# Scores as four wide row tiles, an output projection in 64-row pairs, and new orders, in a two-layer attention and MLP kernel

## The chip, the cores and the metric

The kernel runs on one core of a Trainium2 chip. The metric is the device time of one execution in microseconds (us). The kernel before was timed three times, and the median counts. A profile of one further execution gives, for every instruction, when it began and how long it took. TensorE (PE in the profile, its weight loads PEld) multiplies matrices into PSUM; VectorE (DVE), ScalarE (ACT) and GpSimd (POOL) do the rest; SyncE (SP) issues the DMAs.

## The reference

```
x = x + A(layernorm(x));  x = x + B(layernorm(x))      # both twice, with the same weights
A: qkv = x @ wqkv                    # 2048 x 576 by 576 x 1728, 32 heads of 18
   scores = q k^T * 18**-0.5         # key within the last 256 positions, causal
   p = softmax(scores);  o = p v;  return o @ wo       # wo: 576 x 576
B: y = layernorm(x);  h = gelu(y @ w1 + b1)            # w1: 576 x 4608
   return h @ w2 + b2                                  # w2: 4608 x 576
```

There are 2048 tokens of 576 features, in bf16.

## The kernel before, in words

The 16 token tiles of 128 are taken four at a time, so that each of the two layers has four chunks; the chunks are numbered k = 0 to 7. For each chunk the stages are: the first layernorm and a transposed copy of the activations (`ln1`, `ln_norm_T`), Q, K and V (`qkv`), attention in eight head groups of four heads (`E`, with `scores` and `pv`), the output projection with residual and second layernorm (`tail`), and the MLP in three parts (`G_part` for the first matrix with GELU, `mm2` for the second). The stages of neighbouring chunks are interleaved.

**Tilings of TensorE.** Four shapes are used. QKV of chunks 2 and later and the first MLP matrix run as pairs: two matmuls of 64 rows x 128 columns side by side, on the lower and the upper half of the rows, each into its own PSUM bank (lines 838 and 1077; mode `h`). They run in two phases of 5 and 4 chunks of rows; in the second the halves swap banks, and a flag `own` makes it wait until the first has finished. The second MLP matrix and the output projection use all 128 rows (`two_out`, `quad`; mode `c`): full 128x128 matmuls (line 779), or four 128x32 ones side by side (line 782) where they share a stretch with the product of probabilities and V (`pv`, line 957), which uses that tiling. The scores (line 908; mode `r`) use 32 rows, since a head has 18 features padded to 32: for each of the four heads of a group two matmuls of 32 rows x 64 columns, eight side by side, called a volley in this text. One unit of scores has 512 columns in one or two volleys, for chunks 0 and 4 partly less; a group of four heads has three units. ScalarE takes the exponential (line 919), GpSimd masks the corner blocks (line 940).

**Output projection.** The attention output `attq` holds four head families of 144 features each on the four partition quarters. VectorE transposes it in 32-column chunks into `attT` (line 978). Of the fifth chunk only 16 of 32 columns are real; the rest is set to zero once, as is the fifth chunk of the weights `wo_sb`. So the projection of one token tile takes five row chunks for each of two output halves of 288 columns.

**Order.** The instructions aren't in the order in which the code names them. A planner (`Plan.schedule`) holds a task for each piece of work with an assumed cost, its engine, a priority and what it reads and writes. It takes, again and again, the task that can begin first; among those that begin alike the one with the lowest priority number. A table, `PL.nudge`, adds a number to the priority of every stage and part. A change of tiling on TensorE is charged 0.095 us, and `PL.turn` holds back a task of another tiling by up to 0.3 us. The order so found is fixed in the program for every engine, the DMA queue of SP included. Where TensorE would stand idle early on, the planner puts in zero matmuls (`keep_warm`, line 681); it divides the planned gap by 0.115 us for each.

**Ramp.** Until the first MLP matmul, at 89 us, there is only the attention of chunks 0 and 1 and QKV of chunks 0 to 2. The results of QKV are copied out of PSUM by VectorE (lines 859 and 846), for Q and K of chunk 0 half by ScalarE (line 856). The normalisation ahead of each MLP (`xn`, line 719) is done by VectorE; GpSimd copies its last 64 columns once more (line 727), and a DMA transposes it into `xnTm` (line 742).

Of the kernel before, what the change touches and what calls it, by code (L numbers as in the profile page):

```python
# [7 lines left out]
ACT = mybir.ActivationFunctionType  # L8
# [178 lines left out]
class Plan:  # L187
# [21 lines left out]
    def add(self, eng, fn, reads=(), writes=(), dma=None, ring=4, cost=0.1, lat=0.1, prio=0.0, alloc=(), fifo=None, plain=False, after=(), move=0.0, desc=0, hold=False, mode="f", own=False, port=None, wide=None):  # L209
# [3 lines left out]
        prio += self.nudge.get(stage, 0.0)  # L213
# [35 lines left out]
    def keep_warm(self, a, b, bank_free, extra):  # L249
# [3 lines left out]
        n = int((b - a - 0.1) * 0.8 / 0.115)  # L253
# [5 lines left out]
        t = Task(idx=-1, eng="pe", fn=lambda e: self.warm_fn(e, h.no, n), reads=("warm",), writes=(h,), cost=n * 0.115, lat=0.1, prio=0.0,  # L259
# [175 lines left out]
def build_kernel(nc, A_x, A_wqkv, A_wo, B_x, B_w1, B_b1, B_w2, B_b2, out):  # L435
# [42 lines left out]
    PL.nudge = {"": -58.92, "b": 20.48, "ea0.0": -239.22, "ea0.1": 16.47, "ea0.2": -7.62, "ea0.p0": -24.76, "ea0.p1": -56.2,  # L478
# [105 lines left out]
    def bank(i):  # L584
        if isinstance(i, Bank):
            i = i.no
        return ps[:, i * 512:(i + 1) * 512]
# [123 lines left out]

    xn_ctr = [0]

    def ln_norm_T(t, i, dst, dname, prio, src=None, srcres=None, dup=False, pe=False):
# [602 lines left out]
```

## Time and profile before

| | |
|---|---|
| time, median of 3 runs | 874.53 us (872.73 to 874.58) |
| the profiled execution: span from first to last instruction | 871.0 us |
| what lies around the span, against the median | 3.5 us |
| TensorE busy | 854.1 us (98%), 13464 matmuls |
| its weight loads | 533.0 us |
| ScalarE, VectorE, GpSimd busy | 595.7, 392.3, 376.8 us |
| granted TensorE clock, in 40 slices | 9 tenths or more in each |
| DMA | 120 MB, mean 138 GB/s |

For the profiled execution the span is all that the profile tells of its own time. The span runs from the first instruction to the last; the time of a run has a little more around it. Busy time is the union over an engine's instructions. Matmuls overlap (one of 288 columns is on record for 0.287 us, and the next begins 0.12 us later), so that what a matmul costs TensorE is read from the distance of the starts, not from its length. A row of the timeline has the start, the length from the first start to the last end, the engine, the line, what is written and read, the tiling (rows*columns) and shape, and the count; in brackets stands the idle time before it. A row of groups has, after the bar, busy us and mean ns of one, and then the idle time before, with what ended it. "issue" is waiting for nothing that the profile shows.

### The profile page before, as it was taken

To read this page: it belongs to the slowest core of one execution; us is meant where nothing else is said; L and a number is where in the kernel's file an instruction comes from. 1 tells how busy PE (TensorE), PEld (TensorE's weight loads), DVE (VectorE), ACT (ScalarE), POOL (GpSimd) and SP (SyncE) were. 2 spreads that over 40 slices of the span, in tenths; PEclk is the share of its full clock that TensorE was granted. 3 is DMA by queue.
4 is the path that set the end of the run, shared out by engine and by line. 5 is a ranking of instruction groups with operands and counts; after the bars stand their busy time and mean duration, and the time that the engine had idled before them with its cause. 6 is when DMAs were issued, how large, how long until landed. Compare 5 with 4: busy or idle time off the path is not lost.

```text
span 871.0 us, 30752 instructions
## 1 busy us (share of the span) xinstructions
PE 854.1 (98%) x13464; PEld 533.0 (61%) x13464; DVE 392.3 (45%) x934; ACT 595.7 (68%) x741; POOL 376.8 (43%) x560
## 2 busy tenths in 40 slices
PE   8899999999999999999999999999999999999998
PEld 6556556666556665665655665756556656556556
DVE  4889324554327542384424822654234434234012
ACT  4986788768666588573875776737797589772730
POOL 3876454464144643254421763425454276222100
PEclk9999999999999999999999999999999999999999
DMA  9598435371574715947349453684526963445320
GB/s 238 137 201 143 121 124 149 102 166 44 165 161 118 170 43 164 203 91 166 88 145 222 99 129 124 103 186 99 172 93 136 280 147 105 138 149 156 123 82 28
DMA packets 181877, 120.01 MB, mean 138 GB/s; under 512 B 107440, under 2 KB 181744, under 8 KB 181744
## 3 DMA queue, kind: packets, MB, share of 16 engines
q1 hardware_dynamic: 181744, 118.05, 54.7%
q8 instruction: 106, 1.74, 0.8%
q14 instruction: 27, 0.22, 0.1%
HBM read 90.10 MB, written 2.36 MB: 106 GB/s over the span
## 4 chain that ended last, share of the span: by engine, by line
PE 90%; ACT 3%; DMA 3%; issue 2%; DVE 1%; POOL 0%; DVEq 0%; POOLq 0%
PE ps L1077 32%; PE ps L779 26%; PE ps L782 10%; PE ps L838 9%; PE ps L908 7%; PE ps L957 4%; ACT pT L919 3%; DMA xnTm<-xn 2%; PE ps L798 1%; PE ps L681 1%; DMA x_res<-qn 1%; DMA qT<-qn 1%; DVE xn L719 0%; DVE qn L859 0%; ACT hT L1087 0%
## 5 line engine op out<-in xcount | busy, mean ns | idle before, releaser
L940 POOL TENSOR_SCALAR_AFFINE_SELECT pT<-pT 128x512 bf16<-128x512 bf16 (+1 forms) x368 | 282.8, 789 | 262.8 <-ACT pT L919 260.2
L919 ACT ACTIVATE pT<-ps 128x1024 bf16<-128x1024 f32 (+1 forms) x384 | 347.5, 970 | 62.1 <-PE ps L908 61.1
L1077 PE MATMUL ps<-xnTm,w_sb 64*128 64x512 bf16 x2592 | 290.6, 376 | 2.9 <-DMA xnTm<-xn 2.4
L1087 ACT ACTIVATE hT<-ps,b1col 128x512 bf16<-128x512 f32 x276 | 167.6, 688 | 176.8 <-PE ps L1077 176.3
L1077 PEld LDWEIGHTS ps<-xnTm,w_sb 64*128 64x128 bf16 x2592 | 129.6, 94 | 143.7 <-issue 8.2
L779 PE MATMUL ps<-w_sb,hT 128*128 128x288 bf16 x1410 | 188.8, 287 | 0.0
L1020 DVE TENSOR_TENSOR x_res<-ps,x_res 128x288 f32<-128x288 f32 x224 | 100.2, 451 | 191.9 <-PE ps L779 163.2
L779 PEld LDWEIGHTS ps<-w_sb,hT 128*128 128x128 bf16 x1410 | 130.8, 98 | 47.5 <-issue 13.9
L782 PE MATMUL ps<-w_sb,hT 128*32 128x288 bf16 x2808 | 96.2, 286 | 0.8 <-issue 0.7
L838 PE MATMUL ps<-wqkv,xnTa 64*128 64x288 bf16 x1296 | 91.4, 283 | 0.9 <-DVE x_res L1020 0.6
L968 DVE STREAM_TRANSPOSE oq<-ps 128x512 f32<-128x512 f32 x64 | 45.7, 715 | 101.6 <-PE ps L957 100.8
L859 DVE CAST qn<-ps 128x288 bf16<-128x288 f32 x120 | 48.9, 451 | 81.4 <-PE ps L838 71.7
L782 PEld LDWEIGHTS ps<-w_sb,hT 128*32 128x32 bf16 x2808 | 72.4, 97 | 15.7 <-issue 5.0
L838 PEld LDWEIGHTS ps<-wqkv,xnTa 64*128 64x128 bf16 x1296 | 63.0, 94 | 28.3 <-issue 2.9
L908 PE MATMUL ps<-qT,kT 32*64 32x384 bf16 (+2 forms) x2432 | 69.1, 284 | 3.5 <-DMA qT<-qn 1.5
L694 DVE BATCH_NORM_STATS2 st_all<-x_res 128x6 f32<-128x288 f32 (+1 forms) x128 | 53.5, 443 | 6.9 <-DMA x_res<-in_A_x_dram 6.1
L1093 POOL TENSOR_TENSOR x_res<-x_res,b2bc 128x576 f32<-128x576 f32 x32 | 40.2, 1275 | 34.8 <-ACT hT L1087 34.8
L846 DVE CAST vA<-ps 128x288 bf16<-128x288 f32 x64 | 26.7, 451 | 61.1 <-PE ps L838 59.0
L707 POOL TENSOR_SCALAR vtmp<-mv_all 128x1 f32<-128x1 f32 (+1 forms) x43 | 8.8, 205 | 101.9 <-DVE mv_all L698 99.1
L908 PEld LDWEIGHTS ps<-qT,kT 32*64 32x64 bf16 x2432 | 25.4, 102 | 44.1 <-issue 29.4
L957 PE MATMUL ps<-pT,vA 128*20 128x384 bf16 (+2 forms) x1408 | 50.4, 275 | 1.2 <-POOL pT L940 0.6
L957 PEld LDWEIGHTS ps<-pT,vA 128*20 128x20 bf16 x1408 | 28.2, 91 | 18.1 <-issue 5.5
(58 smaller groups left out, 483.9 us busy)
## 6 DMA issues: line engine op xcount, KB each, us to landing
w_sb<-in_B_w_dram SPq DMA_DIRECT2D x46, 864.0 KB, 5.9
w_sb<-in_B_w_dram SPq DMA_DIRECT2D x48, 768.0 KB, 4.7
w_sb<-in_B_w_dram SPq DMA_DIRECT2D x96, 48.0 KB, 4.5
wqkv<-in_A_wqkv_dram SPq DMA_DIRECT2D x3, 576.0 KB, 5.5
x_res<-in_A_x_dram SPq DMA_DIRECT2D x3, 576.0 KB, 4.9
wqkv<-in_B_w_dram SPq DMA_DIRECT2D x2, 864.0 KB, 6.4
out_dram<-x_res SPq DMA_DIRECT2D x12, 144.0 KB, 2.0
wo_sb<-in_A_wo_dram SPq DMA_DIRECT2D x4, 144.0 KB, 2.6
```

What stands on the lines that cost most here:

```text
L694: add("dve", lambda e, i=i, s=s: e.bn_stats(st_all[:, t, i, :], s[:, t, i * HB:(i + 1) * HB]), reads=res, writes=[f"st{t}_{i}"], cost=0.37 ...
L779: return e.matmul(bank(b)[:, 0:HB], lhs, rhs, start=start, stop=stop, skip_group_check=True)
L782: ins = e.matmul(bank(b)[32 * j:32 * j + 32, 0:HB], lhs[:, 32 * j:32 * j + 32], rhs, start=start, stop=stop, tile_position=(0, 32 * j), sk ...
L838: ins = e.matmul(bank(bs[o])[:, 0:HB], xnTa[r:r + 64, c, i * 128:(i + 1) * 128], wqkv[r:r + 64, c, col:col + HB], start=(c == 4), stop=(ph ...
L859: add("dve", lambda e, b=bs[o], dst=dst: e.tensor_copy(dst, heads_of(bank(b))), reads=[bs[o]], writes=[f"qn{sl}h{o}"], cost=0.375, lat=0.1 ...
L908: ins = e.matmul(two(bs[j // 2])[64 * u:64 * u + 64, j % 2, col:col + nq * 128], k_of(T0 + so)[0][32 * j:32 * j + 32, g, 64 * u:64 * u + 6 ...
L919: add("act", lambda e, h2=h2: e.activation(pT[:, sl, 2 * h2:2 * h2 + 2, lo:hi], two(bs[h2])[:, :, lo:hi], ACT.Exp, scale=SCALE), reads=[bs ...
L940: add("pool", lambda e, ap=ap, pat=pat, sgn=sgn, kind=kind: e.affine_select(ap, ap, pattern=pat, compare_op=(ALU.is_ge if kind == "d" else ...
L957: ins = e.matmul(bank(bo)[32 * j:32 * j + VW, qo * 128:(qo + nq) * 128], vA[:, (T0 + so) % VS, 8 * j + g, :], pT[:, sl, j, col:col + nq * ...
L1020: add("dve", lambda e: e.tensor_tensor(x_res[:, t, sl], bank(b)[:, 0:HB], x_old[:, t, sl], ALU.add), reads=[b] + ([f"xin{t}"] if first els ...
L1077: ins = e.matmul(bank(bks[i])[:, 0:n], w1_sb[r:r + 64, sls[i], col:col + 128], xnTm[r:r + 64, k % 2, c, 0:n], start=(c == 4), stop=(ph == ...
L1087: add("act", lambda e, ff=ff, hd=hd, bk=bk: e.activation(hd[:, 0:n], bank(bk)[:, 0:n], ACT.Gelu_apprx_tanh, bias=b1col[:, ff:ff + 1]), rea ...
```

## The change

- **Scores:** for each head one matmul of 32 rows x 128 columns instead of two of 32x64. A volley is then four matmuls, and writes the same four PSUM banks.
- **Output projection:** pairs of 64x128 in two phases, as QKV does it. The fifth row chunk holds the 64 real features densely, twice: on the lower half for the first output half, on the upper half for the second. So the first phase has five pairs and the second four. VectorE makes the dense copy with four small copies after the last head group; the fifth chunk of the weights comes in eight DMAs instead of four, 12 in all instead of 8. Two memsets go.
- **Zero matmuls:** where a planned gap begins before 8 us, it is divided by 0.2 instead of 0.115.
- **Drains in the ramp:** in chunk 2 ScalarE copies the second half of Q, K and V out of PSUM. For the first MLP (chunk 0) it also does the normalisation, as scale and bias; GpSimd works out the bias first.
- **Orders:** all of `PL.nudge` has new numbers; priorities are rounded to three places.

```diff
@@ keep_warm
-        n = int((b - a - 0.1) * 0.8 / 0.115)
+        each = 0.2 if a < 8.0 else 0.115
+        n = int((b - a - 0.1) * 0.8 / each)
@@ build_kernel
-    PL.nudge = {"": -58.92, "b": 20.48, "ea0.0": -239.22, "ea0.1": 16.47, "ea0.2": -7.62, "ea0.p0": -24.76, "ea0.p1": -56.2,
...
+    PL.nudge = {"": -86.31, "b": 23.63, "ea0.0": -264.23, "ea0.1": 170.66, "ea0.2": 170.75, "ea0.p0": -91.12, "ea0.p1": 0.1, "ea0.p2":
...
-    add("pool", lambda e: e.memset(attq[:, :, 8 * DH:KD * 32], 0.0), writes=["aqd"], cost=0.5, prio=-8)
-    add("dve", lambda e: e.memset(wo_sb[:, 4, :], 0.0), writes=[f"woB{j}" for j in range(4)], cost=0.4, prio=-8)
@@ ln_norm_T
+        if onact:
+            add("pool", lambda e: e.tensor_scalar(vtmp[:, t:t + 1], mv_all[:, t, 0:1], rstd[:, t:t + 1], -1.0, op0=ALU.mult, op1=ALU.mult),
+                reads=[f"mv{t}", f"rstd{t}"], writes=[f"vt{t}"], cost=0.2, lat=0.09, prio=prio)
+            add("act", lambda e: e.activation(xn[:, sl, 0:D], s[:, t, :], ACT.Identity, bias=vtmp[:, t:t + 1], scale=rstd[:, t:t + 1]),
+                reads=res + [f"vt{t}", f"rstd{t}"], writes=[f"xn{sl}"], cost=0.56, lat=0.17, prio=prio)
@@ qkv
+                    if k == 2 and o == 1:
+                        add("act", lambda e, dst=dst, src=src: e.copy(dst, src()), reads=[bs[o]], writes=[f"v{sv}h{o}"], cost=0.32, lat=0.17, prio=prio)
...
-                    if k == 0 and o == 1:
+                    if k in (0, 2) and o == 1:
@@ scores
-                    for u in range(2):
-                        ins = e.matmul(two(bs[j // 2])[64 * u:64 * u + 64, j % 2, col:col + nq * 128],
-                                       k_of(T0 + so)[0][32 * j:32 * j + 32, g, 64 * u:64 * u + 64],
-                                       qs[32 * j:32 * j + 32, g, qo * 128:(qo + nq) * 128], start=True, stop=True, tile_position=(32 * j, 64 * u),
-                                       skip_group_check=True)
+                    ins = e.matmul(two(bs[j // 2])[:, j % 2, col:col + nq * 128], k_of(T0 + so)[0][32 * j:32 * j + 32, g, :],
+                                   qs[32 * j:32 * j + 32, g, qo * 128:(qo + nq) * 128], start=True, stop=True, tile_position=(32 * j, 0),
+                                   skip_group_check=True)
@@ pv
+        if g == G - 1:
+            for p0, p1, c0, w, q0 in ((0, 32, 16, 16, 32), (32, 64, 0, 16, 64), (32, 64, 16, 16, 96), (64, 128, 0, 32, 0)):
+                add("dve", lambda e, p0=p0, p1=p1, c0=c0, w=w, q0=q0: e.tensor_copy(attq[p0:p1, 0:4 * nt, 128 + c0:128 + c0 + w],
+                                                                                   attq[q0:q0 + p1 - p0, 0:4 * nt, 128:128 + w]),
+                    reads=[f"aq{g}"], writes=["aqd"], cost=0.2, lat=0.14, prio=prio - 3, port=True)
@@ tail
-            bs = two_out(lambda c, i=i: attT[:, c, i * 128:(i + 1) * 128], lambda c, s: wo_sb[:, c, s:s + HB],
-                         [f"aT{c}" for c in range(KD)] + [f"wo{x}{j}" for x in "AB" for j in range(4)], prio, mode="c")
+            bs = [Bank(FILL), Bank(FILL)]
+            for ph in range(2):
+                def half(e, ph=ph, bs=bs, i=i):
+                    ins = None
+                    for c in ((0, 1, 2, 3, 4) if ph == 0 else (0, 1, 2, 3)):
+                        for o in ((0, 1) if ph == 0 else (1, 0)):
+                            r = 64 * (o ^ ph)
+                            col = o * HB if c < 4 else 0
+                            ins = e.matmul(bank(bs[o])[:, 0:HB], attT[r:r + 64, c, i * 128:(i + 1) * 128], wo_sb[r:r + 64, c, col:col + HB],
+                                           start=(ph == 0 and c == 0), stop=(ph == 1 and c == 3), tile_position=(r, 0), skip_group_check=True)
+                    return ins
+                add("pe", half, reads=[f"aT{c}" for c in range(KD)] + [f"woA{j}" for j in range(4)] + [f"woB{j}{b}" for j in range(4) for b in range(2)],
+                    writes=bs, cost=mm_cost(HB) * (5 - ph) + 0.01, lat=0.22, prio=prio, mode="h", own=(ph == 1), alloc=(bs if ph == 0 else ()))
...
-            ln_norm_T(t, i, xnTm[:, k % 2], f"xm{k % 2}_", prio, dup=True)
+            ln_norm_T(t, i, xnTm[:, k % 2], f"xm{k % 2}_", prio, dup=True, onact=(k == 0))
@@ wo_load
-            dma("sp", wo_sb[32 * j:32 * j + 16, 4, :], A_wo[r + 128:r + 144, :], reads=["aq0"], writes=[f"woB{j}"], cls="wo", cost=0.6)
+            for b in range(2):
+                dma("sp", wo_sb[64 * b + 16 * j:64 * b + 16 * j + 16, 4, 0:HB], A_wo[r + 128:r + 144, b * HB:(b + 1) * HB], reads=["aq0"],
+                    writes=[f"woB{j}{b}"], cls="wo", cost=0.6)
```

More of the change, by code (lines that the diff above doesn't have):

```diff
@@ L258, in keep_warm @@
         h.no = banks[0]
-        t = Task(idx=-1, eng="pe", fn=lambda e: self.warm_fn(e, h.no, n), reads=("warm",), writes=(h,), cost=n * 0.115, lat=0.1, prio=0.0,
+        t = Task(idx=-1, eng="pe", fn=lambda e: self.warm_fn(e, h.no, n), reads=("warm",), writes=(h,), cost=n * each, lat=0.1, prio=0.0,
                  dma=None, ring=4, alloc=(), handles=(), plain=False, move=0.0, desc=0, fifo=None, hold=False, stage="", mode="f", own=False, port=False, wide=None)
@@ L712, in build_kernel, with ln_norm_T @@
     xn_ctr = [0]
[L714 removed]
+    def ln_norm_T(t, i, dst, dname, prio, src=None, srcres=None, dup=False, pe=False, onact=False):
         s = x_res if src is None else src
@@ L718, in ln_norm_T @@
         xn_ctr[0] += 1
-        add("dve", lambda e: e.tensor_scalar(xn[:, sl, 0:D], s[:, t, :], mv_all[:, t, 0:1], rstd[:, t:t + 1],
-                                              op0=ALU.subtract, op1=ALU.mult),
-            reads=res + [f"mv{t}", f"rstd{t}"], writes=[f"xn{sl}"], cost=0.5 if src is None else 0.37, lat=0.14, prio=prio, port=True)
+        if onact:
[3 more added lines that the diff above has]
+                reads=res + [f"vt{t}", f"rstd{t}"], writes=[f"xn{sl}"], cost=0.56, lat=0.17, prio=prio)
+        else:
+            add("dve", lambda e: e.tensor_scalar(xn[:, sl, 0:D], s[:, t, :], mv_all[:, t, 0:1], rstd[:, t:t + 1],
+                                                  op0=ALU.subtract, op1=ALU.mult),
+                reads=res + [f"mv{t}", f"rstd{t}"], writes=[f"xn{sl}"], cost=0.5 if src is None else 0.37, lat=0.14, prio=prio, port=True)
         rd = [f"xn{sl}", f"xd{sl}"]
@@ L845, in qkv @@
                 for o in range(2):
[L846 to L848 removed]
+                    dst, src = vA[:, sv, o * 16:(o + 1) * 16, 0:DH], lambda b=bs[o]: bank(b)[:, 0:HB].rearrange("p (h d) -> p h d", d=DH)
+                    if k == 2 and o == 1:
+                        add("act", lambda e, dst=dst, src=src: e.copy(dst, src()), reads=[bs[o]], writes=[f"v{sv}h{o}"], cost=0.32, lat=0.17, prio=prio)
+                    else:
+                        add("dve", lambda e, dst=dst, src=src: e.tensor_copy(dst, src()), reads=[bs[o]], writes=[f"v{sv}h{o}"], cost=0.375, lat=0.14,
+                            prio=prio)
             else:
@@ L978, in pv @@
                 add("dve", lambda e, c=c: e.transpose(attT[:, c, 0:nt * 128], attq[:, 0:4 * nt, 32 * c:32 * c + 32]),
-                    reads=[f"aq{x}" for x in range(32 * c // DH, g + 1)] + ["aqd"], writes=[f"aT{c}"], cost=0.6, lat=0.14, prio=prio - 3)
+                    reads=[f"aq{x}" for x in range(32 * c // DH, g + 1)] + (["aqd"] if c == 4 else []), writes=[f"aT{c}"], cost=0.6, lat=0.14, prio=prio - 3)
     def E0(gs, prio):
```

7 lines of the change are left out of this document (2 added, 5 removed), and 134 rows, old and new, of the table add.

## The prediction

> **What bounds the kernel now.** I read the page first (busy shares, then the chain that ended last).
>
> ```profile
> span 871.0 us, 30752 instructions
> PE 854.1 (98%) x13464; PEld 533.0 (61%) x13464; DVE 392.3 (45%) x934; ACT 595.7 (68%) x741; POOL 376.8 (43%) x560
> PE 90%; ACT 3%; DMA 3%; issue 2%; DVE 1%; POOL 0%; DVEq 0%; POOLq 0%
> ```
>
> TensorE is busy for 98% of the span and holds 90% of the chain. Work taken from it shortens the kernel wherever no other engine is the limit at that moment. The table by stage shows where one is:
>
> ```profile
> core 0: us, PE busy (x) PEld busy (x) DVE busy (x) ACT busy (x) POOL busy (x), PEclk, DMA share, GB/s
> 30.00:60.00 30.00, 27.57 (x539) 16.21 (x537) 23.68 (x55) 27.81 (x38) 25.34 (x38) 1.00 0.88 174
> 60.00:90.00 30.00, 26.98 (x478) 16.86 (x480) 27.15 (x65) 20.18 (x21) 20.01 (x35) 1.00 0.90 173
> 600.00:700.00 100.00, 100.00 (x1603) 60.62 (x1602) 39.53 (x91) 75.71 (x91) 46.17 (x63) 1.00 0.61 156
> ```
>
> From 30 to 60 us ScalarE is full (27.81 of 30), from 60 to 90 VectorE (27.15 of 30). Later, as in 600 to 700, TensorE alone is full. The longest waits of TensorE are few:
>
> ```profile
> PE ps L1077 <- DMA xnTm<-xn: 2.4, 2, 2.0
> PE ps L908 <- DMA qT<-qn: 1.5, 1, 1.5
> ```
>
> So new orders have little waiting to win back; what counts is the time the instructions themselves take on TensorE. That has to be read from starts, because matmuls overlap and busy time hides the slots. The timeline of TensorE, with start, length and count:
>
> ```profile
> 70.81 0.37 PE L908 MATMUL ps<-x_res,xnTm 32*64 32x384 bf16 x8
> 71.00 0.24 PE L908 MATMUL ps<-x_res,kT 32*64 32x128 bf16 x8
> 71.17 2.38 PE L838 MATMUL ps<-wqkv,xnTa 64*128 64x288 bf16 x36
> 73.84 2.62 PE L779 MATMUL ps<-wo_sb,attT 128*128 128x288 bf16 x20
> 76.39 0.42 PE L908 MATMUL ps<-x_res,kT 32*64 32x256 bf16 x16
> 785.54 11.92 PE L779 MATMUL ps<-w_sb,hT 128*128 128x288 bf16 x96
> 797.39 0.39 PE L1077 MATMUL ps<-xnTm,w_sb 64*128 64x512 bf16 x2
> ```
>
> And the groups, with mean ns after the busy time:
>
> ```profile
> L779 PE MATMUL ps<-wo_sb,attT 128*128 128x288 bf16 x255 | 33.8, 287 | 0.1
> L782 PE MATMUL ps<-wo_sb,attT 128*32 128x288 bf16 x260 | 8.6, 286 | 1.6 <-issue 1.6
> L908 PE MATMUL ps<-qT,kT 32*64 32x384 bf16 x896 | 41.5, 345 | 2.7 <-DMA qT<-qn 1.5 <-ACT pT L919 0.9 <-ACT kT L876 0.3
> L908 PE MATMUL ps<-qT,kT 32*64 32x128 bf16 x768 | 23.2, 214 | 0.5 <-issue 0.5
> ```
>
> 96 full matmuls of 288 columns take 11.92 us and the last alone 0.287: a slot is (11.92 - 0.287)/95 = 0.1225 us, or 0.425 ns a column. The 20 matmuls from 73.84 end their slots at 76.29 and the next tiling starts at 76.39: changing the tiling costs 0.10 us. The 36 pair matmuls from 71.17 hold 18 slots, so pairs of 64 rows run side by side.
>
> **Output projection** (tail, L1041 to L1047). Before, each of 32 token tiles has 5 chunks x 2 halves = 10 slots; the rows show 255 full matmuls and 260 in groups of four, 320 slots. After, the first phase has 5 pairs and the second 4, 9 slots. 32 x 0.1225 = **-3.9 us**. The second phase swaps the row tiles between the same two banks and so waits for the first (own). The pair form of QKV (L838) does that already; who waited for it (us, times), and the group of its weight loads, which gives 1296/18 = 72 tasks:
>
> ```profile
>   PE ps L838: 1.5, 4
> L838 PEld LDWEIGHTS ps<-wqkv,xnTa 64*128 64x128 bf16 x1296 | 63.0, 94 | 28.3 <-issue 2.9 <-PE ps L838 1.5 <-DVE x_res L1020 0.9
> ```
>
> The loads waited on their own engine 4 times, 1.5 us in all, 0.38 each; less the 0.12 slot that a pair takes anyway, 0.26. Elsewhere other work stands between. I take the same share, 2 of 32: **+0.5** (0 to +8.3, all 32). Here the Trainium skill, TensorEngine Tiling (Array Packing), section Restrictions and Gotchas, says that different row tiles must not access one PSUM bank at the same time and that software has to see to it. By that rule no tile can skip the ordering; where nothing fills it, the sum is that of the rival below. The four waits agree with it, and the other 68 tasks show that it can be covered.
>
> The tail also changes from the full tiling to that of MLP-1 and QKV. Beside scores (as at 73.84) this alters nothing; beside either family it adds or saves a change. I take **0** (-1 to +3.2, which is two new changes of 0.10 at every second of the 32 tiles).
>
> **Scores** (L908 to L912). Eight tiles of 32x64 become four of 32x128 with the same columns, so the streaming stays. What changes is the stagger. The union of eight 384-column matmuls is 0.37 against 0.345 for one, 0.24 against 0.214 at 128 columns: seven steps, 0.025 us, 3.6 ns each. The next volley starts only behind it: 71.00 - 70.81 = 0.19 where 384 columns stream 0.163. Four steps fewer save 14 ns. By the code, chunks 0 and 4 have 4 volleys a group and the other six chunks 6: 8 x (2 x 4 + 6 x 6) = 352 volleys. The 32 of chunk 0 lie in the stretch that ScalarE fills and count nothing; were that cover gone, they would give 0.4 more. 320 x 14 ns = **-4.5 us** (bounds -8.8, the whole stagger of all 352, to the loss below). Do wide loads keep the 3.6 ns? Three places in the timeline, and the group of the score loads:
>
> ```profile
> 308.43 0.16 PEld L908 LDWEIGHTS ps<-qT,kT 32*64 32x64 bf16 x16 [0.24 <-issue]
> 76.74 0.10 PEld L838 LDWEIGHTS ps<-wqkv,xnTa 64*128 64x128 bf16 x2 [0.20 <-issue]
> 300.25 0.11 PEld L1077 LDWEIGHTS ps<-xnTm,w_sb 64*128 64x128 bf16 x2
> L908 PEld LDWEIGHTS ps<-qT,kT 32*64 32x64 bf16 x2432 | 25.4, 102 | 44.1 <-issue 29.4 <-ACT pT L919 11.5 <-ACT hT L1087 1.9
> ```
>
> Just after a change of tiling two 128-column loads lie within 0.10, at 94 ns each: 4 ns or so apart. In the middle of a run they can stand 0.11 - 0.094 = 16 ns apart. Each score run follows a change of tiling, so I take the first. The Trainium skill, TensorE: Matmul & The Clock Gate, section LDWEIGHTS, has the load time go with the columns, which makes 128 columns (107 ns) twice as dear as 64; exposed once in each of the 192 score runs (3 units x 8 groups x 8 chunks) that would add an estimated 10 us. The two groups of loads, 94 ns for 128 columns (L838) and 102 for 64 (L908), do not agree with it.
>
> **Start.** 29 zero matmuls become 16, since a planned gap is now divided by 0.2 and not 0.115.
>
> ```profile
> 2.18 5.78 SPq L631 DMA_DIRECT2D wqkv<-in_A_wqkv_dram  x9
> 2.72 4.82 PE L681 MATMUL ps<-warm 128*128 128x256 bf16 x29
> 5.18 0.43 DVE L719 TENSOR_SCALAR xn<-x_res,mv_all,rstd 128x576 bf16<-128x576 bf16 x1 [0.72 <-POOL rstd L709]
> 7.38 0.44 PE L736 MATMUL ps<-ident,xn 128*128 128x128 bf16 x5
> 8.65 1.39 PE L798 MATMUL ps<-wqkv,xnTa 128*128 128x288 bf16 x10 [0.28 <-issue]
> wqkv<-in_A_wqkv_dram SPq DMA_DIRECT2D x3, 576.0 KB, 5.5
> ```
>
> xn is there at 5.61, but the transposes wait behind zeros until 7.38. With 16 they could start at about 6.1. The first QKV matmul then meets its weights, issued at 2.18 and landing 5.5 later, at about 7.8 instead of 8.65. The first scores hang on a transposing DMA anyway (a wait of 1.5 us above), so part is lost: **-0.5** (0 to -1.2). The dropped memsets lie off the chain: 0.
>
> **Drains moved to ScalarE** (k = 2 and the first MLP's norm). VectorE loses 8 + 4 casts and 4 normalisations, ScalarE gains them and GpSimd 4 small operations ahead of the normalisations, which on ScalarE's queue stand behind the exponentials that come first:
>
> ```profile
> L859 DVE CAST qn<-ps 128x288 bf16<-128x288 f32 x120 | 48.9, 451 | 81.4 <-PE ps L838 71.7 <-PE ps L798 5.5 <-PE ps L779 2.2
> L856 ACT CAST qn<-ps 128x288 bf16<-128x288 f32 x8 | 3.2, 406 | 3.2 <-PE ps L798 3.2
> L719 DVE TENSOR_SCALAR xn<-x_res,mv_all,rstd 128x576 bf16<-128x576 f32 x48 | 27.3, 576 | 6.0 <-DMA xnTm<-xn 3.8 <-issue 1.2 <-POOL rstd L709 0.8
> L739 ACT COPY xnTa<-ps 128x640 bf16<-128x640 bf16 x4 | 2.8, 696 | 2.0 <-PE ps L736 2.0
> ```
>
> VectorE: -(12 x 0.451 + 4 x 0.576) = -7.7 us of its 27.15. ScalarE: 12 x 0.406 + 4 x 0.7 = +7.7, to 27.9 of 30: full, but just not over. Against it stand four new VectorE copies ahead of each chunk's last transpose (three of 256 columns, one of 512; no row has such a copy; a 512-column pass takes 0.65 below, so at most 4 x 0.65 = 2.6, and by columns 1.6, which I take) and four more output-weight DMAs on SP, 8 of which take 4.25:
>
> ```profile
> 37.55 4.25 SPq L631 DMA_DIRECT2D wo_sb<-in_A_wo_dram  x8
> 42.09 3.24 SPq L878 DMA_TRANSPOSE x_res<-qn  x2
> 775.10 1.30 DVE L978 STREAM_TRANSPOSE attT<-attq 128x512 bf16<-128x512 bf16 x2
> 780.63 5.07 PE L779 MATMUL ps<-wo_sb,attT 128*128 128x288 bf16 x40
> ```
>
> The DMAs (+2.1 us of queue) push the transposes behind them in a stretch that ScalarE fills; uncovered they cost 2.1. The copies have 4.2 us of room in the last chunk (776.4 to 780.63); uncovered they cost 1.6 a chunk. The 2.0 us wait before the first MLP is what the move can shorten: **-1.5** (-3 to +2.1).
>
> **Instruction supply.** The 1.6 us wait at L782 is on nothing that the profile shows, in a stretch of four-way groups of the projection. That form is gone from it, and scores need half their instructions: **-1.5** (0 to -1.6).
>
> **Orders.** All priorities are new. Little waiting is there to win, more to lose: **+1** (-2 to +14).
>
> Sum: -3.9 + 0.5 + 0 - 4.5 - 0.5 - 1.5 - 1.5 + 1 = -10.4, a span of 860.6 us. The median of the runs, 874.53, lies 3.5 above the profiled span; with that the time is 864.1 us.
>
> **Rivals.** (1) The second phase waits in every tile: +8.3 instead of +0.5, 871.9. For it: the wait is in the code. Against: 4 of 72.
> (2) Start, drains and instruction supply give nothing because transfers and ScalarE set the ramp: +3.5, 867.6. For it: DMA share 0.9 there.
> (3) Slower: the wide loads of a volley start 16 to 17 ns apart. Three steps make 51 ns where 25 stand now: +8.3 instead of -4.5, 876.9. It decides from about 14 ns a step (10.4 us over 320 volleys is 32, on top of 11). For it: 300.25. Against: 76.74.
> (4) Slower: later transposed activations. The 2.0 us wait before MLP-1 recurs at the other seven chunks, +14: 878.1. It decides from 1.5 us a chunk. For it: the last chunk's cover, 785.54 + 11.92, ends just where MLP-1 starts (797.39), and the copies lengthen that chain. Against: only one other such wait now.
>
> **How the numbers follow.** The forecast 0.40; (2) 0.14; (1) 0.10; the bounds of scores and start reached together, under 858, 0.08; (3) 0.07; (4) with other losses by order 0.15; a draw within 0.2% (872.8 to 876.3, about what a measurement here can tell from no change) 0.06. Faster 0.72, same 0.06, slower 0.22. The range 858 to 877 leaves out most of the under-858 case and of (4), about 0.19; the forecast's own is 859 to 868.
>
> **What would show it.** Projection rows of 64*128, x576. L908 at 32*128, x1408, the second volley 0.17 to 0.18 behind a 384-column one instead of 0.19. First QKV matmul near 7.9. VectorE near 21 of 30 us in 60 to 90, the wait of L1077 on xnTm shorter. No issue wait at the projection. I am wrong if L1077 waits on xnTm in several chunks, if L908 steps exceed 14 ns, or if weight loads of the projection wait on their own engine in most tiles.

## The result and the profile after

The changed kernel takes 864.99 us (median of four runs, 864.07 to 866.79) where the kernel before takes 873.87 beside it; the measured ratio is 0.9903, 95% interval 0.9886 to 0.9919 (the two medians alone give 0.9898). The forecast was 864.1, in a range of 858 to 877.

Two errors of 1.7 us cancel in that number. The profiled execution took 864.07 us with a span of 862.3, so the forecast span of 860.6 was 1.7 too short. And only 1.8 us lie around the span, not 3.5: the 3.5 came from taking the median of before (874.53) against the span of an execution that itself took 872.73. How the sum came about is therefore a better question than how near it was.

The page of the changed kernel (span, busy shares, the chain that ended last):

```profile
span 862.3 us, 27890 instructions
PE 846.4 (98%) x12002; PEld 520.0 (60%) x12002; DVE 395.7 (46%) x949; ACT 601.2 (70%) x757; POOL 378.6 (44%) x563
PE 88%; DMA 4%; DVE 2%; POOL 2%; ACT 2%; issue 1%; SPq 0%; POOLq 0%; ACTq 0%
```

TensorE still bounds it. 1462 matmuls are gone, yet its busy time fell by only 7.7 us: the matmuls that went had run side by side with others. The table by stage and TensorE's longest waits (us, times, longest):

```profile
core 0: us, PE busy (x) PEld busy (x) DVE busy (x) ACT busy (x) POOL busy (x), PEclk, DMA share, GB/s
30.00:60.00 30.00, 25.99 (x398) 14.96 (x398) 22.75 (x53) 24.58 (x34) 22.19 (x33) 0.94 0.85 138
60.00:90.00 30.00, 27.99 (x463) 16.34 (x464) 20.95 (x53) 27.69 (x39) 22.31 (x41) 1.00 0.90 158
...
PE ps L781 <- DMA xnTa<-xn: 2.6, 1, 2.6
PE ps L778 <- DVE vA L849: 1.6, 2, 1.0
```

From 60 to 90 us VectorE has 20.95 and ScalarE 27.69, against 21 and 27.9 forecast. But from 30 to 60 TensorE is busy for less than before (25.99 against 27.57), waits 2.6 us for a transposing DMA, and its granted clock is 0.94. The old waits, 2.0 us for xnTm and 1.6 us on nothing at the projection, are gone.

The timeline of TensorE (start, length, count) and two groups of weight loads, for the scores (now L909) and the projection (now L1048):

```profile
70.95 0.34 PE L909 MATMUL ps<-x_res,xnTm 32*128 32x384 bf16 x4
71.12 0.22 PE L909 MATMUL ps<-x_res,kT 32*128 32x128 bf16 x4
71.31 2.38 PE L1048 MATMUL ps<-wo_sb,attT 64*128 64x288 bf16 x36
...
L1048 PE MATMUL ps<-wo_sb,attT 64*128 64x288 bf16 x576 | 42.0, 283 | 0.3
...
L1048 PEld LDWEIGHTS ps<-wo_sb,attT 64*128 64x128 bf16 x576 | 27.5, 94 | 14.5 <-PE ps L1048 1.5 <-DVE attT L983 0.6 <-DVE x_res L1025 0.6
L909 PEld LDWEIGHTS ps<-qT,kT 32*128 32x128 bf16 x1216 | 19.4, 92 | 42.7 <-issue 29.8 <-ACT pT L919 11.6 <-DVE attq L974 0.5
```

The projection has 576 pair matmuls, 288 slots for 32 tiles, 9 each. Its loads waited on their own engine four times, 1.5 us in all, where the forecast took two tiles of 32. In these four tiles the second phase starts 0.351 us behind the last pair of the first, in place of a slot of 0.1225: 0.23 us more each, 0.9 in all. The second score volley stands 0.17 behind a 384-column one, where it was 0.19. In the median over all pairs of volleys that begin with 384 columns the starts give 173 ns in place of 187, and from the first matmul of two volleys to the next task 329 in place of 356: 27 ns, where the forecast took 2 x 14. The four matmuls of a volley start 3 to 4 ns apart.

Where the time went is read from three starts. (Two views of before and after: the first MLP matmul, and all between the first score and it.)

```profile
89.13 2.12 PE L1077 MATMUL ps<-xnTm,w_sb 64*128 64x512 bf16 x18 [1.98 <-DMA xnTm<-xn]
...
21.22:89.13 67.91, 61.33 (x1101) 37.39 (x1102) 59.57 (x149) 55.32 (x69) 50.85 (x82) 1.00 0.82 162
```
```profile
89.62 1.69 PE L1093 MATMUL ps<-xnTm,w_sb 64*128 64x512 bf16 x14 [0.73 <-DVE vA L849]
...
20.06:89.62 69.56, 63.05 (x942) 36.81 (x942) 53.08 (x137) 60.58 (x84) 50.80 (x85) 0.98 0.87 156
```

The first score comes 1.2 us earlier (20.06 against 21.22), but that lies within the scatter: over all executions profiled it comes at 20.23 to 21.28 us with 29 zero matmuls (six kernels) and at 20.06 to 22.80 with 16 (eight). The first MLP comes half a microsecond later. So the ramp gained nothing: all of the gain, 9.2 us, lies between the first MLP and the last matmul (778.7 us before, 769.5 after). One place in the ramp stands out, with the timeline of TensorE and of SP's queue there:

```profile
29.43 0.34 PE L909 MATMUL ps<-qT,kT 32*128 32x384 bf16 x4
32.37 0.80 PE L781 MATMUL ps<-wqkv,xnTa 128*32 128x288 bf16 x20 [2.60 <-DMA xnTa<-xn]
...
35.59 2.23 PE L778 MATMUL ps<-wqkv,xnTa 128*128 128x288 bf16 x10
```
```profile
24.52 1.57 SPq L626 DMA_DIRECT2D w_sb<-in_B_w_dram  x3
26.85 7.06 SPq L741 DMA_TRANSPOSE xnTa<-xn  x4
```
```profile
30.52:33.93 3.41, 1.56 (x45) 1.03 (x46) 1.39 (x5) 0.81 (x2) 2.21 (x5) 1.00 0.89 68
33.93:37.35 3.42, 3.42 (x18) 1.73 (x18) 1.58 (x5) 3.02 (x4) 2.33 (x4) 0.50 0.36 71
```

The new order puts three transfers of MLP weights (768 KB and twice 48 KB) on SP ahead of the transposes of chunk 1, which land late; TensorE waits 2.6 us; and right behind, from 33.93 to 37.35, its granted clock is 0.50 (ten matmuls of 288 columns take 2.23 us at L778, where 1.40 is usual). The profiled execution of the kernel before shows no such stretch.

### The profile page after: what moved, and what is told of

It is laid out like the page before. It is cut to its first block, busy times and chain, and to the rows that moved or that the text cites. A ratio compares the mean times of both kernels' runs of the same rounds, so it can differ in the third digit from the quotient of the medians.

```text
span 862.3 us, 27890 instructions
## 1 busy us (share of the span) xinstructions
PE 846.4 (98%) x12002; PEld 520.0 (60%) x12002; DVE 395.7 (46%) x949; ACT 601.2 (70%) x757; POOL 378.6 (44%) x563
## 3 DMA queue, kind: packets, MB, share of 16 engines
q8 instruction: 95, 1.56, 0.8%
## 4 chain that ended last, share of the span: by engine, by line
PE 88%; DMA 4%; DVE 2%; POOL 2%; ACT 2%; issue 1%; SPq 0%; POOLq 0%; ACTq 0%
PE ps L1093 30%; PE ps L778 25%; PE ps L781 10%; PE ps L837 8%; PE ps L909 6%; PE ps L957 4%; PE ps L1048 3%; DMA xnTm<-xn 2%; ACT pT L919 1%; DMA xnTa<-xn 1%; PE ps L797 1%; POOL pT L940 1%; DVE xn L718 1%; DVE x_res L1025 1%; DMA qT<-qn 1%
## 5 line engine op out<-in xcount | busy, mean ns | idle before, releaser
L778 PE MATMUL ps<-w_sb,hT 128*128 128x288 bf16 x1446 | 193.7, 287 | 1.5 <-DVE x_res L1025 0.7
L778 PEld LDWEIGHTS ps<-w_sb,hT 128*128 128x128 bf16 x1446 | 133.6, 98 | 52.6 <-issue 17.1
L781 PE MATMUL ps<-w_sb,hT 128*32 128x288 bf16 x2664 | 91.6, 286 | 0.2
L861 DVE CAST qn<-ps 128x288 bf16<-128x288 f32 x112 | 45.7, 448 | 99.1 <-PE ps L837 88.9
L781 PEld LDWEIGHTS ps<-w_sb,hT 128*32 128x32 bf16 x2664 | 68.4, 97 | 14.9 <-issue 4.6
L909 PE MATMUL ps<-qT,kT 32*128 32x384 bf16 (+2 forms) x1216 | 64.2, 277 | 2.8 <-ACT pT L919 1.6
L909 PEld LDWEIGHTS ps<-qT,kT 32*128 32x128 bf16 x1216 | 19.4, 92 | 42.7 <-issue 29.8
L718 DVE TENSOR_SCALAR xn<-x_res,mv_all,rstd 128x576 bf16<-128x576 f32 (+1 forms) x60 | 34.4, 578 | 21.1 <-DMA xnTm<-xn 9.0
```

Source lines behind the costliest of these rows:

```text
L778: return e.matmul(bank(b)[:, 0:HB], lhs, rhs, start=start, stop=stop, skip_group_check=True)
L781: ins = e.matmul(bank(b)[32 * j:32 * j + 32, 0:HB], lhs[:, 32 * j:32 * j + 32], rhs, start=start, stop=stop, tile_position=(0, 32 * j), sk ...
L861: add("dve", lambda e, b=bs[o], dst=dst: e.tensor_copy(dst, heads_of(bank(b))), reads=[bs[o]], writes=[f"qn{sl}h{o}"], cost=0.375, lat=0.1 ...
L909: ins = e.matmul(two(bs[j // 2])[:, j % 2, col:col + nq * 128], k_of(T0 + so)[0][32 * j:32 * j + 32, g, :], qs[32 * j:32 * j + 32, g, qo * ...
```

## The experiments

Each ratio is to the kernel before on the same chip. Two ratios are compared through it, which leaves about 0.0023, 2 us, either way. Every trace is of one execution.

**Scores alone** (the kernel before, its orders unchanged):

```diff
-for u in range(2):
-    ins = e.matmul(two(bs[j // 2])[64 * u:64 * u + 64, ...], k_of(T0 + so)[0][32 * j:32 * j + 32, g, 64 * u:64 * u + 64], ..., tile_position=(32 * j, 64 * u))
+ins = e.matmul(two(bs[j // 2])[:, ...], k_of(T0 + so)[0][32 * j:32 * j + 32, g, :], ..., tile_position=(32 * j, 0))
```

> The kernel before with the scores alone in the new form; the order of all work stays as it was. Theory (stagger): 320 volleys x 14 ns = -4.5 us, so 869.4 us and a ratio of 0.995; a full unit from its first matmul to the next task goes from 356 to about 329 ns. Rival (the saving is hidden, or the wide loads cost as much): 873.9 us, ratio 1.000; slower, 882, if wide loads start 16 ns apart.

864.67 us, 0.9898 (0.9877 to 0.992): -8.9 us (7.0 to 10.7; the medians alone, 864.67 and 872.60, lie 7.9 apart), twice the forecast and as much as the whole change. The step is 329 ns in place of 356 here too, and the stretch behind the ramp shrinks by 3.5 us (778.7 to 775.2), near the 3.7 that 13.5 ns give for the 272 volleys there. This execution also lost some 1.7 us in that stretch, at half clock (last row) behind a stall of 2.30 us. The rest came in the ramp, where the forecast had struck 32 volleys out because ScalarE fills it. Its first MLP, the stretch from the first score to it, and the half clock:

```profile
84.72 2.55 PE L1075 MATMUL ps<-xnTm,w_sb 64*128 64x512 bf16 x22 [0.17 <-DVE attq L972]
...
20.29:84.72 64.43, 60.44 (x902) 36.70 (x902) 57.22 (x147) 53.65 (x70) 49.55 (x80) 1.00 0.85 168
...
566.19:569.60 3.41, 3.41 (x20) 1.20 (x16) 1.89 (x5) 0.00 (x0) 1.35 (x5) 0.50 0.82 53
```

The first MLP comes 4.4 us earlier; 0.9 of that lies ahead of the first score, where the edit changes nothing. From there the ramp is 3.5 us shorter (64.43 against 67.91). By the stagger alone its 80 volleys would give 1.1. The other 2.4 come with shorter waits: TensorE's for xnTm (2.0 us) is gone and that for qT fell from 1.5 to 0.3 us, and from 20 to 60 us ScalarE waited 1.8 us for scores in place of 3.4. ScalarE is busy for 53.65 of 64.43 us: not full, so "ScalarE fills it", read off a busy share, was wrong. It and TensorE take turns, a score volley, its exponential, a freed bank, the next volley, so that a shorter volley shortens the loop. This fits, but it is argued: no run here separates the loop from the transfers.

**The other way round: the changed kernel with the old scores** (the inverse of that edit).

> The changed kernel with the scores alone put back to eight 32x64 matmuls; order unchanged. Theory: +4.5 us on 865.0, so 869.5, ratio to before 0.995. Rival (in the new order the scores lie in waiting time): 865, ratio 0.990.

0.9967 (0.9952 to 0.9981). Against 0.9903 the scores are worth 0.64%, 5.6 us, here: nearer to 4.5, and by the middle values less than in the old orders. The first MLP comes at 92.15, 2.5 us later, but 1.7 of these lie ahead of the first score; the stretch behind it takes 4.3 us more.

**Projection with its tenth slot back** (one more pair of 64-row matmuls with zero operands a tile):

```diff
+for o in ((1, 0) if ph == 1 else ()):
+    ins = e.matmul(bank(bs[o])[:, 0:HB], attT[r:r + 64, 0, ...], warm[r:r + 64, 0:96]..., start=False, stop=True, tile_position=(r, 0))
```

> The changed kernel with one more pair of matmuls (times zero) at the end of the second phase of each projection tile; order unchanged. It gives back the slot that the packing of the last 64 rows takes away. Theory (each slot of the projection is on the path): 32 x 0.1225 = +3.9 us, 868.9, ratio to before 0.9945. Rival (projection slots fall into waits for their own first phase or for VectorE): under +1, ratio 0.990 to 0.991.

0.9951 (0.9933 to 0.9969): 0.48%, 4.2 us for 32 slots, 0.13 us each. The forecast's 3.9 stands.

**Instruction supply** (the kernel before, its projection in full tiles everywhere, no groups of four):

```diff
+            if t.wide is not None and t.stage[:1] == "t":
+                t.wide[0] = True
```

> The kernel before with every projection matmul in full 128x128 form, none in groups of four; order unchanged, at most two more changes of tiling (0.2 us), 195 fewer matmuls with their loads. Theory (instruction supply): the 1.6 us wait in the projection at 571 us goes and perhaps the 0.9 at 268; -1.4 to -2.3 us, 871.6 to 872.5, ratio 0.9975 to 0.9984. Rival (the wait is a transfer of data or the profile's own): the wait stays or comes a little later, 873.9, ratio 1.000.

0.9969 (0.9954 to 0.9984), -2.7 us. The stall of the kernel before in such a group stands in its timeline (the profile names no releaser):

```profile
569.77 1.51 PE L782 MATMUL ps<-wo_sb,attT 128*32 128x288 bf16 x41
572.85 0.43 PE L782 MATMUL ps<-wo_sb,attT 128*32 128x288 bf16 x7 [1.57 <-issue]
```

Behind the start-up the three kernels in old orders have 11 such stalls of over 0.23 us. Ahead of 10 of them the trace has a packet of the instruction queue, 16 KB, that takes about 1 us and starts 2.2 to 3.1 us before the stall ends; with 106 packets in 871 us a stretch of 0.9 us holds one by chance one time in nine. In us:

```
kernel        stall ends  its length  packet starts  between
before             68.28        0.24          65.22     3.1
before            268.90        0.85         266.29     2.6
before            572.85        1.73         570.66     2.2
before            757.66        0.68         755.23     2.4
scores alone      263.57        0.98         261.03     2.5
scores alone      387.68        0.24         382.24     5.4
scores alone      489.21        0.46         486.70     2.5
scores alone      565.25        2.30         562.64     2.6
full tiles        206.45        0.38         203.97     2.5
full tiles        272.24        1.15         269.62     2.6
full tiles        569.19        0.60         566.19     3.0
```

So it looks as if TensorE runs out of instructions where many short ones stand in a row, and goes on 2 to 3 us after the next piece has begun to come. That is inferred from the times of the packets; no run changes the supply alone. With full tiles no such stall is left at the projection, and their sum falls from 3.5 us to 2.1. The changed kernel has none at all (two gaps of 0.26 us named "issue", at 35.16 and 35.59, lie at half clock). But fewer score instructions alone do not help (scores alone: four stalls, 4.0 us), and the sum differs between executions: the kernel before with fewer zero matmuls (below) has two, idle for 1.42 and 0.14 us. That the time falls is clear (2.7 us, 1.3 uncertain); that the stalls make up 1.4 of it rests on one execution each.

**Scores and full tiles together**, in the old orders.

> The kernel before with two edits, in its own orders: scores as one matmul a head, and the projection in full 128 row tiles everywhere in place of groups of four. Apart they gave 0.9898 and 0.9969. If they add: 0.987, about 861 us, faster than the changed kernel, and no idle time without a cause at the projection. Rival: half the score instructions already took the stall of instructions away, so that the second edit adds only the tiling changes saved: 0.989 to 0.990.

863.02 us, 0.9888 (0.9865 to 0.991). Two edits of a few lines, without new orders, give what the whole change gives. Whether the second adds to the first is not resolved: 0.001 between them, 0.003 uncertain.

**The drains back on VectorE** (the 12 copies of chunk 2 and the 4 normalisations, in the same places of the same order):

```diff
-add("act", lambda e, dst=dst, src=src: e.copy(dst, src()), ...)
+add("dve", lambda e, dst=dst, src=src: e.tensor_copy(dst, src()), ...)
```

> The changed kernel with the 12 copies of chunk 2's q, k and v and the 4 normalisations of chunk 0's first MLP back on VectorE, in the places of the same order; the 4 small GpSimd operations ahead of the normalisations go. The prediction: they are worth 1.5 us, so the time rises by 1.5 us, ratio 0.992, VectorE at 27 to 29 of 30 us in the stretch of 60 to 90, and TensorE waits there for v or the normalised rows. Rival 1 (the drains give nothing, since other stages set the ramp): first MLP within 0.5 us of 89.6, ratio 0.990. Rival 2 (ScalarE was the fuller engine, the move did harm): the first MLP comes 1 to 2 us earlier and the ratio falls to 0.988.

0.9956 (0.9939 to 0.9974): 0.53%, 4.6 us, about 2 uncertain: more than the 1.5 forecast, though not clear of its bound of 3. The stretch 60 to 90, TensorE's waits, and VectorE just ahead of the last of them:

```profile
60.00:90.00 30.00, 27.45 (x447) 15.12 (x447) 26.11 (x67) 19.26 (x22) 21.74 (x36) 1.00 0.85 159
...
PE ps L789 <- DMA xnTa<-xn: 2.5, 1, 2.5
PE ps L786 <- DVE vA L858: 2.1, 2, 1.1
PE ps L786 <- DVE x_res L1036: 1.8, 3, 1.1
PE ps L968 <- DVE x_res L1036: 1.6, 1, 1.6
...
177.62 0.43 DVE L726 TENSOR_SCALAR xn<-x_res,mv_all,rstd 128x576 bf16<-128x576 bf16 x1 [2.69 <-DMA xnTm<-xn]
```

VectorE has 26.11 again. The first MLP is 1.7 later (0.6 of it ahead of the first score), the stretch behind it 3.5 longer. There TensorE waits more for x_res, which VectorE writes: 3.4 us in these two rows, 1.1 in the changed kernel, between 170 and 700 us. The work that was moved had ended by then (at 91 us in the changed kernel), and VectorE's load is not the cause of the longest, 1.61 us at 178.64: VectorE had itself stood 2.69 us for a transposing DMA (last row), and was busy for 18.45 of the 30 us from 150 to 180. How a change in the ramp lengthens what lies behind it is open. Part of it may be the test's own: the order was made for drains on ScalarE.

**29 zero matmuls again** (the changed kernel, the old divisor):

```diff
-        each = 0.2 if a < 8.0 else 0.115
+        each = 0.115
```

> The changed kernel with the divisor of the planned gaps at 0.115 again, so 29 and 5 zero matmuls in place of 16; all orders stay. The prediction: the first QKV matmul goes back from 7.6 to about 8.6 us, and half of that microsecond is lost at the end, +0.5 us or +0.06% against the changed kernel, a ratio of 0.991. Rival: the 1.0 us is swallowed whole by the wait for chunk 1's transposed activations at 32 us, which ends on transfers: the first MLP stays at 89.6 within 0.3 us, and the ratio at 0.990. Second rival: it is lost whole, +1.1 us, first MLP at 90.7, ratio 0.9916.

862.19 us (861.76 to 862.51), 0.9871 (0.9856 to 0.9886). None of the three expectations: with more zeros it is faster, by 2.8 us (about 2 uncertain), and has the lowest median of the study. The start of this kernel, then of the changed one:

```profile
2.72 3.90 PE L674 MATMUL ps<-warm 128*128 128x256 bf16 x29
6.46 0.44 PE L735 MATMUL ps<-ident,xn 128*128 128x128 bf16 x5
7.73 1.39 PE L797 MATMUL ps<-wqkv,xnTa 128*128 128x288 bf16 x10 [0.28 <-ACT xnTa L738]
```
```profile
2.72 3.62 PE L674 MATMUL ps<-warm 128*128 128x256 bf16 x16
6.13 0.68 PE L735 MATMUL ps<-ident,xn 128*128 128x128 bf16 x5
7.64 1.39 PE L797 MATMUL ps<-wqkv,xnTa 128*128 128x288 bf16 x10 [0.50 <-ACT xnTa L738]
```

29 zeros took hardly longer than 16, 0.134 us each against 0.226: the full clock came earlier in this execution. So the first QKV was hardly later (7.73 against 7.64). And the clock did not fall at 34 us:

```profile
31.92 0.80 PE L781 MATMUL ps<-wqkv,xnTa 128*32 128x288 bf16 x20 [1.85 <-DMA xnTa<-xn]
...
33.93:37.35 3.42, 3.22 (x61) 1.96 (x58) 2.27 (x8) 3.42 (x6) 3.10 (x4) 1.00 0.64 125
```

A stretch of 3.41 us at half clock takes 0.002 off the mean clock of an execution. All four executions of this kernel have 1.000; of the changed kernel's four, three have 0.998 and one 0.996. Its price is seen within one kernel, the one with the tenth slot: 866.1 to 867.2 us at 1.000 (3 executions), 868.1 to 869.4 at 0.998 (4), 869.9 to 871.9 at 0.996 (3), some 2 us a stretch, where 3.41 us at half speed lose 1.7. The four executions of the changed kernel have five such stretches, 1.25 each, so by this estimate 2.1 to 2.5 of the 2.8 us are the clock. Why the wait was shorter with 29 zeros (1.85 against 2.60, one execution each) is open.

**Fewer zeros alone** (the kernel before with the new divisor).

> The kernel before with the divisor 0.2 for gaps ahead of 8 us: fewer zero matmuls at the start (16 and 2 or 3 in place of 29 and 5), nothing else. The prediction's term: -0.5 us, ratio 0.9994 (bounds 0.9986 to 1). Rival: fewer zeros do harm by themselves, as the changed kernel with 29 again was 2.8 us faster: +1.5 to +2.8 us, ratio 1.002 to 1.003. If it is within 0.1% of 1, the harm in the changed kernel came from what stands behind, the wait for xnTa and the clock.

1.0009 (0.998 to 1.0038): nothing that this run can tell, in either direction; -0.5 is inside. Its executions scatter more than others: three of twelve took 878.6 to 880.6 us at a mean clock of 0.994, three stretches of half clock by the reckoning above, where none of the 56 executions of the kernel before that ran beside the tests lies under 0.996. The other nine took 868.3 to 874.4. Whether the missing zeros bring the stretches is not shown.

**The weights behind the transposes** (the changed kernel, three transfers moved on SP):

```diff
+        moved = [x for x in order if x[1].dma == "w1" and x[1].stage == "ld0+"]
+        order = [x for x in order if x not in moved]
+        order[last + 1:last + 1] = moved   # last: the fourth transpose of xnTa, chunk 1
```

> The changed kernel with one move: the three transfers of the first MLP's weights that stand on SP's queue ahead of the four transposing transfers of chunk 1's activations are put behind them; every instruction and every other order stays. Theory: the 2.6 us wait of TensorE for xnTa at 32.4 us, and the half clock from 33.9 to 37.4 us that follows it, come from that transfer and lengthen the ramp. Then the wait goes, the clock stays full, the first MLP starts 2.5 to 4.5 us earlier than 89.6 us, and the time against the changed kernel falls by 2.5 to 4.5 us, to a ratio of 0.985 to 0.988 against the kernel before. Rival: ScalarE and the transfers fill the ramp as a whole, so that the wait only moves on to the weights of the first MLP or to the next transposes: the first MLP stays within 1 us of 89.6, and the ratio at 0.990.

0.9913 (0.9894 to 0.9932): no gain, the rival holds. The wait at 32 us is gone and the clock stays at 1.00 in the profiled execution, yet the first MLP starts at 90.00. Its first score came 1.1 us later (21.16), so that from there the ramp is 0.7 us shorter (68.84 against 69.56), where 2.5 to 4.5 were expected. The rest of the gain was given back at 66 us: TensorE is done with its pv group at 64.70 (64.03 + 0.67), and the next scores start only at 65.96. Timeline of TensorE, of SP, and the last transfer's time to landing:

```profile
64.03 0.67 PE L961 MATMUL ps<-pT,vA 128*20 128x384 bf16 x16
65.96 0.34 PE L913 MATMUL ps<-x_res,xnTm 32*128 32x384 bf16 x4 [1.27 <-issue]
...
59.66 1.23 SPq L884 DMA_TRANSPOSE xnTm<-qn  x1
...
xnTm<-qn SPq DMA_TRANSPOSE x1, 6.2
```

Those scores read xnTm, which here holds transposed keys of chunk 1; 59.66 + 6.2 = 65.86. In the changed kernel the same transfer is issued at 59.37 and takes 6.1, to 65.47, and its scores start at 65.56. The profile says "issue", no instruction packet lies there, and the transfer ends where the stall does: that it is the transfer is inferred. So what is won at 32 us meets a transfer at 65.9 that does not come earlier.

**Zeros in the wait** (the changed kernel, 12 zero matmuls ahead of the waiting QKV group):

```diff
+        order.insert(at, (..., Task(eng="pe", fn=lambda e: self.warm_fn(e, h.no, 12), ...)))   # at: first QKV group of chunk 1
```

> The changed kernel with 12 more zero matmuls (about 0.107 us each at full clock) on TensorE's queue directly ahead of the first QKV group of chunk 1, where TensorE waits 2.6 us for xnTa; nothing else is moved. Theory: the half clock from 33.9 to 37.4 us comes from that idle time, and costs about 1.7 us (3.41 us at half speed). Then the wait is shortened to about 1.4 us without the transfer landing earlier, the clock stays full, and the time falls by about 1.7 us against the changed kernel, ratio 0.988 to 0.989. Rival 1: the clock falls for another reason; it falls here too, ratio 0.990 to 0.991. Rival 2: the clock stays full, but what follows waits for ScalarE and VectorE instead, first MLP within 0.5 us of 89.6 us, ratio 0.990.

0.99 (0.9877 to 0.9923), 863.62 us: no gain that can be told. The clock did what the theory says: no fall at 34 us in the profiled execution, 1.000 in four of six (0.998 in the profiled one, from a wait of 2.55 us for the first weights). The four took 862.3 to 863.8 us, the two others 865.0 and 866.1. From the first score to the first MLP it took 67.56 us in place of 69.56.

```profile
32.45 1.48 PE L679 MATMUL ps<-warm 128*128 128x256 bf16 x12
35.04 0.80 PE L786 MATMUL ps<-wqkv,xnTa 128*32 128x288 bf16 x20 [1.11 <-DMA xnTa<-xn]
```

**Both: 29 zeros, and the weights behind.**

> The changed kernel with both edits, 29 and 5 zero matmuls at the start and the weights' transfers behind the transposing ones. Theory: with the zeros the clock no longer falls in the ramp, so that the 1.8 us wait for xnTa is left to win; taken away, the ratio falls from 0.987 to 0.985 or 0.986. Rival: as with the transfers alone the waiting moves on to the copies of v and q, the exponentials' banks and the instructions' own arrival, and the ratio stays at 0.987 (or up to 0.989, if moving the weights does harm).

0.9892 (0.987 to 0.9915): nothing on top of the zeros; its profile has the same stall, up to 66.09. The rival holds again.

**The old orders** (the changed kernel, planned with the table of priorities of before).

> The changed kernel planned with the table of priorities of the kernel before; the instructions stay the same in number and kind, only their orders change. The prediction's term for the new table is +1 us (-2 to +14) for the table of after; so with the old table the time would be 0 to 2 us lower, a ratio of 0.988 to 0.990. Rival: the table of after is fitted to the new instructions, and the old one brings waits of 2 to 8 us, a ratio of 0.992 to 1.0; then those waits stand in the ramp (first MLP later than 91 us), or in waits of MLP-1 and projection behind it, where the stretch from the first MLP to the end would be over 772 us.

949.82 us, 1.0877: +77 us against before, far outside both expectations. Its waits, and its mean granted clock:

```profile
PE ps L915 <- ACT pT L925: 18.9, 30, 1.3
PE ps L915 <- DMA kT<-qn: 12.0, 3, 8.8
PE ps L963 <- POOL pT L946: 7.8, 4, 4.0
...
core 0: 950.1 us, clock 0.968
```

The old table, planned with the new tasks, makes a plan that falls apart. It tells that new orders were needed, and nothing of what they cost by themselves. That term was not measured.

## Why the prediction was right, and where it was not

The time was right, by a sum of terms of which several were wrong. That it lay so near is in part luck: the span fell by 8.7 us where 10.4 were forecast, and the 3.5 us taken for what lies around it, in place of 1.8, made up for that.

- **Output projection**, -3.9 + 0.5: right. 288 slots; 4.2 us by the zero pair; four waits of 0.23 us, 0.9 for the 0.5, so rival (1) falls. Changes of tiling, put at 0, went from 416 to 410. The rule of the Trainium skill that was weighed there (TensorEngine Tiling (Array Packing), Restrictions and Gotchas) agrees with the four gaps, and the other 28 tiles show that it can be covered.
- **Scores**, -4.5: the mechanism and its size were right, 27 ns for two volleys, and rival (3) falls: the wide loads start 3 to 4 ns apart. A load of 128 columns takes 92 ns, where one of 64 took 102. The step that failed is "the 32 of chunk 0 lie in the stretch that ScalarE fills and count nothing": the forecast priced the stagger alone, and no wait that a shorter volley shortens. In the old orders the ramp gained 3.5 us from the first score on, and the edit was worth 8.9; in the new ones 5.6.
- **Start**, -0.5: the trace did what was forecast (transposes at 6.13 for 6.1, first QKV at 7.64 for 7.8), the time did not. The step that failed is the delay itself: it was read from one execution, whose 29 zeros took 4.82 us, and in another they took 3.90. The first score comes no earlier with 16 than with 29. In the old orders no gain can be told, and in the changed kernel the fewer zeros cost 2.8 us (2 uncertain), most of it by the clock as estimated above, which the term left out.
- **Drains**, -1.5: right in sign and in the busy times of both engines, mis-sized: 4.6 us by the test (2 uncertain). The forecast priced the wait before the first MLP alone; 3.5 us of what the test's execution lost lie behind it, in waits whose cause is open.
- **Instruction supply**, -1.5: borne out in sign and, within the uncertainty, in size: full tiles gave 2.7 us (1.3 uncertain), and no such stall is left in the changed kernel's execution. The packets point to the cause. Of the two reasons given, the second, half the score instructions, did not take the stalls away by itself.
- **Orders**, +1 (-2 to +14): not measured alone. By the rest: the tests give 0.64 + 0.48 + 0.53% for scores, projection and drains and -0.32% for the start, 1.33% in all, against 0.97% measured; so 0.36%, some 3 us, may have been lost by new orders and by terms that do not add. Taken together the tests are uncertain by 0.6%, so that this loss is not shown. What the new orders did bring is the wait at 32 us and the half clock, which the forecast did not see: it looked for losses at xnTm (rival 4), where there are none. Taking the wait away gained nothing that can be told.
- **Rival (2)**, that start, drains and supply give nothing: wrong for drains and supply; for the start no gain was found.

## What to carry to other kernels

A busy share near full does not say that an engine fills a stretch: where two engines take turns over few buffers, shortening the work of one may shorten the loop (argued here, not shown). Try the piece of a change with the plainest mechanism alone, in the old orders: here one matmul for two was worth the whole change. Read the time of a first event from several executions before pricing it: the first score here came anywhere from 20.1 to 22.8 us. In a ramp bounded by transfers, time won ahead of one transfer is kept only if the next comes earlier too, so look for the next before pricing the first.

## What was not expected of the hardware

A wait of 2.6 us of TensorE was followed by 3.42 us at a granted clock of 0.50, and one of 1.85 by none. But a wait of 2.52 us at the same place, in the kernel with the tenth slot, was followed by none either:

```profile
32.46 0.80 PE L781 MATMUL ps<-wqkv,xnTa 128*32 128x288 bf16 x20 [2.52 <-DMA xnTa<-xn]
...
30.69:34.10 3.41, 1.64 (x46) 1.10 (x47) 1.47 (x5) 0.84 (x3) 2.21 (x5) 1.00 0.68 61
34.10:37.51 3.41, 3.21 (x51) 2.01 (x53) 2.42 (x7) 3.41 (x5) 2.72 (x4) 1.00 0.57 111
```

So the length of the wait does not decide alone. The falls lie on a grid: whole steps of 3.413 us from where the clock first became full (6.62 us in the changed kernel, whose fall at 33.93 is eight steps on; 6.79 in this one). In the step ahead of its fall TensorE was busy for 1.56 us in the changed kernel, and here for 1.64. In the thirteen traces other than that of the old orders, every step at full clock with 1.56 us of work or less (six of them) is followed by one at half clock, and none with 1.64 or more is; in the old orders falls come up to 1.73 us of work. So it depends on how a wait falls on the grid, which begins elsewhere in each execution.

The Trainium skill, TensorE: Matmul & The Clock Gate, section What's actually happening, puts the return to half speed after an idle window of about 3.4 us, free-running. The length of the stretch agrees (3.42); the idle time does not, as TensorE was busy for 1.56 of the 3.41 us ahead of it.

Full clock came as early as 3.88 us and as late as 6.79 in the executions profiled, so that 29 zero matmuls can take hardly longer than 16 (3.90 against 3.62 us).

A piece of 16 KB of instructions takes about 1 us to arrive, and TensorE stood still for up to 2.3 us around it.
